# Weight conversion in an attention and MLP kernel: four raw buffers, conversions laid across two pairs, and another queue for stores of x's rows

## Chip, cores and metric

The kernel runs on one core of a Trainium2 chip. The metric is the device time of one execution in microseconds (us), lower is better. A core has five engines with instruction streams of their own: TensorE (PE in the profile; its weight loads are PEld), VectorE (DVE), ScalarE (ACT), GpSimd (POOL) and SyncE (SP), which here only issues DMA transfers. ScalarE and GpSimd can issue them too. "SPq L252" in a profile is an instruction of SyncE's queue from line 252 of the kernel. A queue is worked off in order: an instruction that waits holds up all behind it.

## What is computed

An attention block in which each query sees only the keys of its own cluster, and then a feed-forward block with a residual. Cut to what matters:

```python
def _attn_ref(q, k, v, centroids):          # q, k, v: (4, 8, 768, 64) float32
    q_assign = argmax(q_n @ c_n)            # 16 clusters for each head
    k_assign = argmax(k_n @ c_n)
    mask = q_assign[:, :, :, None] == k_assign[:, :, None, :]
    scores = where(mask, scale * q @ k.T, -1e9)
    return softmax(scores) @ v

def _moe_ref(x, g_ln, w_ch1, w_ch2):        # x: (4, 768, 512)
    xn = (x - mean(x)) / sqrt(var(x) + 1e-06) * g_ln
    return x + maximum(xn @ w_ch1, 0) @ w_ch2
```

The inputs are float32, except the weights `w_ch1` (512 x 2048) and `w_ch2` (2048 x 512). These reach the kernel as 64-bit floating-point numbers. The kernel reads them as pairs of 32-bit words and puts float32 weights together with integer operations.

## The kernel before

**Attention.** The work goes by 16 pairs of heads (4 batches, 4 pairs each); L740 is the loop over the pairs, `n` its index. For each pair TensorE makes masks and scores (L398), ScalarE the exponentials (L393), TensorE the weighted sums of v (L410). VectorE adds the exponentials up (L445 to L449), transposes q and k (L295) and finds the clusters. For batches 0 and 1 `rows_out` (L513) also transposes a pair's result and stores it as rows of x to `x_d` in four DMAs of 96 KB; for batches 2 and 3 this waits until later, and only the columns are stored, to `xT_d` (L504).

**Conversion of the weights.** There are 32 chunks of 128 x 512 weights: 0 to 15 of `w_ch1`, 16 to 31 of `w_ch2`. `load_weight(m)` (L244) brings a chunk's raw words, 512 KB, into a buffer with the tag "raw" (4 KB on each of 128 partitions). `split_weight(m)` (L259) is three VectorE instructions (L265, L268, L271). `join_weight(m)` (L275) is two (L282, L283) and a DMA from GpSimd's queue that adds the low part onto the float32 weight (L286, `w<-tb`). After the join the raw buffer is free, and the call that follows loads chunk m + 2 into it, as there are two raw buffers. In the attention `weight(n, part)` (L733) converts one chunk in each of the pairs 0 to 14, and a second one at the end of the pairs in `TWICE`. That makes 19 chunks; the other 13 are converted in the first stage of the MLP.

**The MLP of batch 0, first layer** (`first_units`, L1325). Each product of matrices is done by a scheme with seven half-size products instead of eight. A unit `j` is seven products of four matmul records; units 1 to 7 follow each other. VectorE adds up the weights that the next unit needs as `ws` (`w1_sums`, L646, instructions at L658), adds PSUM results (L876), and converts the chunks that the list in L841 gives the unit: one in unit 1, two in each of the units 2 to 7. Here the raw, "ta" and "tb" buffers lie in a pool `rest` (L832).

**The MLP of batch 0, second layer** (L1362 to L1421). Seven parts of three row tiles each (L953). `add_rows` (L960) loads a tile of x's rows (`xb`, four buffers) and adds it to the product into `o_sb` (tag "o", nine buffers). In between come jobs for the next batches. Among them `turn_columns` (L1375) transposes a pair of batch 2 or 3 from columns (`col`) to rows (`turned`, one buffer) and stores it with four DMAs (L518). These tiles live in a pool `early`.

**The MLP of batches 1 to 3.** Units as before (L1490), and behind each unit of batch 1 `unit_end` (L1428) turns the remaining pairs and prepares quarter blocks of the second layer's weights (`w2_split`, L1046, instructions at L1053; its source for the blocks 4, 5, 6 and 7 comes back from DRAM by `w2_back`, L1030, into a single buffer). `leaving` (L1188) is a list of stores whose DMA instructions are issued later, by `leave(n)` (L1204).

**Order.** A `manual_schedule` fixes the order on the engines it names as the program has it; on others a scheduler orders the instructions by simulated time. SyncE's order is fixed in the first lines of the attention (L691) and from L1423 on, and left to the scheduler in the attention's loop, in the first layer of batch 0 and in the second layer of batch 0. ScalarE's is left to it only in the second layer of batch 0. The pools lie on a stack in SBUF: `rest` is closed at L1364, and `ffn` and `early` are opened in its place and beyond. A tile there waits until what lay at its place before is no longer used.

Of the kernel before, what the change touches and what calls it, by code (L numbers as in the profile page):

```python
# [8 lines left out]
F32 = mybir.dt.float32  # L9
# [14 lines left out]
def kernel(  # L24
# [11 lines left out]
    nc = tc.nc  # L36
    B, H, S, D = q.shape
    NCL = centroids.shape[1]
    DM, FF = moe_w_ch1.shape
    P = 128  # L40
# [14 lines left out]
    xpool = ctx.enter_context(tc.tile_pool(name="xpool", bufs=1))  # L55
# [10 lines left out]
    conv = pool("conv", 1)  # L66
# [13 lines left out]


    LATER = 2
    TWICE = (1, 10, 11, 12)


    def load_blocks(n, name):
# [142 lines left out]
    WC = 512  # L229
    NW1 = NDC * FF // WC  # L230
    NWC = NW1 + NFC
    raws = {}
    least = const.tile([P, NWC], F32, name="least")
    limit = [NWC]
# [9 lines left out]
    def load_weight(m):  # L244
        if m < NWC and m < limit[0]:
            if limit[0] < NWC:

                raw = xpool.tile([P, 4, NDH, P], F32, tag="ws", name="raw", bufs=2)
                raw = raw.rearrange("p i c f -> p (i c f)").bitcast(mybir.dt.int64)
            else:  # L250
                raw = pools["conv"].tile([P, WC], mybir.dt.int64, tag="raw", name="raw", bufs=2)
            nc.sync.dma_start(out=raw, in_=weight_chunk(m)[0])  # L252
            raws[m] = raw

# [255 lines left out]
        else:  # L510
            late.pop(n)

    def rows_out(b, pr, x, y):  # L513

        nc.vector.transpose(y, x)
        for i in range(P // Q):
            m = pr * P + i * Q
            nc.sync.dma_start(  # L518
                out=x_d[b].rearrange("t (a r) m -> r (t a) m", r=Q)[:, :, m : m + Q],
                in_=y[i * Q : (i + 1) * Q].rearrange("r (g f) -> r g f", f=Q),  # L520
            )
# [2 lines left out]
    asked = list(turning)  # L524
    columns = {}

    def columns_load(tile_of):
        if asked:
            b, pr = asked.pop(0)
            columns[b, pr] = tile_of()  # L530
            nc.sync.dma_start(out=columns[b, pr], in_=xT_d[b][pr])

    def columns_turn(tile_of):
        b, pr = turning.pop(0)
        rows_out(b, pr, columns.pop((b, pr)), tile_of())


    stat_d = [spill.tile([2, S], F32, name=f"stat_d{b}") for b in range(B)]
# [143 lines left out]

    convert = {}
    for n in range(len(pairs) - 1):
        for part in (0, 1) if n in TWICE else (0,):
            convert[n, part] = len(convert)

    pieces = [(0, 0, 0), (1, 0, 0), (1, 1, 0), (0, 1, 0), (1, 0, 1), (1, 1, 1), (0, 0, 1)]
# [34 lines left out]
    with tc.manual_schedule(engines=order | {mybir.EngineType.Pool}):  # L723
        def extras(n, at):
            for job in extra.pop((n, at), ()):
                job()

        def turn_pair(n):
            for side in (1, 0):
                prep_transpose(n, side)  # L730
                load(n + 1, "qk"[side])

        def weight(n, part):  # L733
            m = convert.get((n, part))
            if m is not None:
                split_weight(m)
                join_weight(m)
                load_weight(m + 2)

        for n in range(len(pairs)):  # L740
            nxt = n + 1 < len(pairs)
            own = range(2 * NT * n, 2 * NT * (n + 1))
            if n == 0:
                turn_pair(1)
            elif nxt:
                prep_route(n + 1)
            load(n + 1, "v")
            for i in own:
                if i >= AHEAD:
                    scores(i)  # L750
                if n == 0 and i + 1 == NT:
                    prep_sims(1)
                    prep_route(1)
            extras(n, "scores")
            if 1 < n and nxt:
                finish(n - 2, 1)
            if n and n + 2 < len(pairs):
                turn_pair(n + 2)
            if not nxt:
                finish(n - 1, 1)  # L760
            add_up(n, 0)
            extras(n, "sums")
            if not nxt:
                finish(n - 2, 2)
                finish(n - 2, 3)
            if n and nxt:
                finish(n - 1, 0)
            if nxt:
                for piece in pieces[:4]:
                    prep_mask(n + 1, *piece)  # L770
            add_up(n, 1)
            if n == 0:
                turn_pair(2)
            for i in own[:NT]:
                weigh(i)
            if nxt:
                for piece in pieces[4:]:
                    prep_mask(n + 1, *piece)
            weight(n, 0)
            if n > 1 and nxt:  # L780
                finish(n - 2, 2)
                finish(n - 2, 3)
            extras(n, "weigh")
            for i in own[NT:]:
                weigh(i)
            if n + 2 < len(pairs):
                prep_sims(n + 2)
            elif nxt:
                finish(n, 0)
            weight(n, 1)  # L790
            extras(n, "end")
            if n + 2 == len(pairs):
                finish(n - 1, 1)
            if not nxt:
                for part in (2, 3):
                    finish(n - 1, part)
# [34 lines left out]
    rest, first = ExitStack(), ExitStack()  # L831
    pools["conv"] = rest.enter_context(tc.tile_pool(name="rest", bufs=1))  # L832
    limit[0] = NWC
    for m in range(len(convert), min(len(convert) + 2, NWC)):
        load_weight(m)

    within = {}
    for m in range(len(convert), NWC):
        within.setdefault((1, 2, 2, 3, 3, 4, 4, 5, 5, 6, 6, 7, 7)[m - len(convert)], []).append(m)
    MH = DM // 2  # L840
    hidden = {}  # L841

# [117 lines left out]
    def add_rows(b, r, tt, j, bank):  # L960

        x = early.tile([P, MH], F32, tag="xb", name="xb", bufs=4)
        nc.sync.dma_start(out=x, in_=x_d[b][r * TH + tt, :, j * MH : (j + 1) * MH])
        o = early.tile([P, MH], F32, tag="o", name="o_sb", bufs=9)
        nc.vector.tensor_tensor(o, bank[:, :MH], x, ALU.add)
        return o

# [236 lines left out]
    def leave(n, queues=(nc.sync,)):  # L1204
        for i, (to, y) in enumerate(leaving[:n]):
            queues[i % len(queues)].dma_start(out=to, in_=y)
        del leaving[:n]
# [117 lines left out]
    def first_units(b, j):  # L1325

        chunks = within.pop(j, []) if b == 0 else []
        for part, ahead in ((1, 0), (2, 0), (4, 1), (6, 0), (3, 1), (5, 0), (7, 0)):
# [6 lines left out]
            if chunks and part in (2, 3):  # L1335
                m = chunks.pop(0)
                join_weight(m)
                load_weight(m + 2)

            if part == 5 and j + 1 < NFH:  # L1340
                w1_sums(b, j + 1)
# [20 lines left out]
    with tc.manual_schedule(engines={mybir.EngineType.PE, mybir.EngineType.DVE}):  # L1362
# [10 lines left out]
            return early.tile([P, S], F32, tag="col", name="col", bufs=2)  # L1373

        def turn_columns():  # L1375
            columns_turn(lambda: early.tile([P, S], F32, tag="turned", name="turned", bufs=1))
            if len(turning) > 4:
                columns_load(column)

        def keep(i, t):  # L1380
            return lambda: w2_keep(i, st["t", t])
# [41 lines left out]
    with tc.manual_schedule(engines=order | {mybir.EngineType.SP}):  # L1423
# [4 lines left out]
        def unit_end(b, j):  # L1428
# [4 lines left out]
                if j < NT:  # L1433
                    norm_rows(b + 1, j)
            if b == 1:
                def row():
                    return xpool.tile([P, S], F32, tag="row", name="col", bufs=2)

                if turning and j % 2:
                    columns_turn(row)  # L1440
                elif asked and j % 2 == 0:
                    columns_load(row)
                if j == 0:
                    outer["ends"] = all_in_range()
                if j == 2:
# [17 lines left out]
            if b + 1 < B and j + 2 == NFH:  # L1463
                norm_stat_rows(b + 1)
            leave(4)
            if j > 4:
                for _ in range(4):
                    if ring["next"] < len(STEPS) * (b - 1) + RING:
                        ring_load(b)
# [261 lines left out]
```

## Time and profile before

| what | value |
|---|---|
| three runs | 904.64, 903.95, 903.05 us; median 903.95 us |
| the profiled execution | 904.72 us, of which the instructions' span is 902.8 us |
| TensorE clock granted, mean | 0.993 of full |
| busy: PE, PEld, DVE, ACT, POOL | 97%, 64%, 78%, 45%, 9% |
| DMA | 151.01 MB, 167 GB/s mean |

The span by stage (us of the span; busy us of the engines; the mean busy share of the 16 DMA engines):

| stage | from, to | length | PE | DVE | ACT | PE clock | DMA |
|---|---|---|---|---|---|---|---|
| attention | 0, 318.3 | 318.3 | 315.5 | 286.3 | 256.7 | 1.00 | 0.78 |
| batch 0, first layer | 318.3, 409.0 | 90.7 | 81.8 | 64.6 | 26.7 | 0.96 | 0.69 |
| batch 0, second layer | 409.0, 480.8 | 71.8 | 69.4 | 52.5 | 2.4 | 1.00 | 0.70 |
| batch 1, first layer | 480.8, 557.8 | 77.0 | 75.8 | 58.8 | 35.8 | 1.00 | 0.70 |
| the rest | 557.8, 902.8 | 345.0 | 334.1 | 242.4 | 81.2 | 0.99 | 0.53 |

TensorE is busy nearly all the time, so other engines' time counts only where TensorE waits for it. A line of a timeline has the start in us, the length in us, the engine, the source line, the operation, the tiles written and read, their shape and the number of instructions; in brackets stands how long the engine had been idle before it, and what ended that.

### The profile page before, as it was taken

The page shows a single profiled execution, that of the slowest core. Times are in us where ns is not written, and L with a number is a line of the kernel's source. Part 1 is how long each engine was busy: PE and PEld are TensorE (multiplying, and loading weights), DVE is VectorE, ACT ScalarE, POOL GpSimd, SP SyncE. Part 2 cuts the span into 40 slices and gives each one's busy share as a digit, 9 for nine tenths or more (in the row PEclk, how much of TensorE's full clock was granted, in tenths as well). Part 3 has the DMA queues.
Part 4 walks back from the last instruction along what each step waited for, and adds up shares of the span by engine and source line. Part 5 has one row for each costly group of instructions (what it writes and reads, how often), then busy time and mean ns, then how long its engine had stood idle before and what let it go on. Part 6 is the DMA issues. An engine that isn't in the chain of part 4 may idle for free.

```text
span 902.8 us, 13188 instructions
## 1 busy us (share of the span) xinstructions
PE 876.6 (97%) x4644; PEld 575.4 (64%) x4644; DVE 704.5 (78%) x1149; ACT 402.8 (45%) x739; POOL 77.4 (9%) x143
## 2 busy tenths in 40 slices
PE   9999999999999998989989999999999999999995
PEld 5444444444444455548876556997557997557995
DVE  6899998999998876868657887897646897645774
ACT  6777889888898623221002552102553101333110
POOL 1022111112222202110000000000000000000000
PEclk9999999999999999999999999999999999999998
DMA  7777989988994247867675778963235862421874
GB/s 160 137 145 137 168 153 192 172 168 173 196 195 130 66 150 193 247 170 235 172 185 164 230 232 284 330 196 88 50 84 170 286 204 59 86 84 36 269 201 94
DMA packets 251642, 151.01 MB, mean 167 GB/s; under 512 B 193696, under 2 KB 209200, under 8 KB 250544
## 3 DMA queue, kind: packets, MB, share of 16 engines
q1 hardware_dynamic: 235936, 133.90, 56.7%
q0 software_dynamic: 7776, 15.03, 8.4%
q10 hardware_dynamic: 7856, 1.16, 0.8%
q8 instruction: 39, 0.64, 0.3%
q14 instruction: 35, 0.29, 0.1%
HBM read 108.40 MB, written 33.25 MB: 157 GB/s over the span
## 4 chain that ended last, share of the span: by engine, by line
PE 81%; DVE 7%; DMA 7%; SPq 2%; issue 2%; ACT 1%; DVEq 0%; ACTq 0%; POOLq 0%
PE s_ps L398 16%; PE x_ps L845 13%; PE a_ps L410 13%; PE x_ps L1136 12%; PE z_ps L845 7%; PE z_ps L1136 6%; PE y_ps L845 3%; DMA raw<-in_moe_w_ch_dram 3%; PE y_ps L1136 3%; PE x_ps L953 2%; PE den_ps L466 1%; PE sim_ps L317 1%; PE y_ps L953 1%; PE z_ps L953 1%; DVE lower L876 1%
## 5 line engine op out<-in xcount | busy, mean ns | idle before, releaser
L398 PE MATMUL s_ps<-t,t 64*128 64x384 f32 x768 | 154.8, 483 | 0.0
L398 PEld LDWEIGHTS s_ps<-t,t 64*128 64x128 f32 x768 | 68.0, 187 | 39.0 <-issue 38.3
L1136 PE MATMUL x_ps<-lower,w 128*128 128x192 f32 x448 | 80.9, 327 | 0.9 <-DVE u L1151 0.9
L1136 PEld LDWEIGHTS x_ps<-lower,w 128*128 128x128 f32 x448 | 74.0, 190 | 2.9 <-DVE u L1151 1.5
L876 DVE TENSOR_TENSOR lower<-z_ps,u 128x384 f32<-128x384 f32 x56 | 31.0, 553 | 52.7 <-PE z_ps L845 45.1
L884 ACT ACTIVATE lower<-lower 128x384 f32<-128x384 f32 x88 | 45.5, 522 | 59.0 <-DVE lower L876 59.0
L393 ACT ACTIVATE e<-s_ps 128x768 f32<-128x768 f32 x84 | 67.0, 811 | 7.0 <-PE s_ps L398 6.4
L393 ACT ACTIVATE w<-s_ps 128x768 f32<-128x768 f32 x80 | 64.4, 811 | 8.3 <-PE s_ps L398 7.7
L398 PE MATMUL s_ps<-mask,mask 64*128 64x384 bf16 x384 | 62.8, 323 | 1.0 <-ACT e L393 0.6
L871 ACT COPY u<-x_ps 128x384 f32<-128x384 f32 x64 | 30.5, 477 | 64.6 <-PE x_ps L845 64.6
L410 PE MATMUL a_ps<-e,v_sb 128*64 128x384 f32 x336 | 57.6, 488 | 0.0
L871 ACT COPY p<-x_ps 128x384 f32<-128x384 f32 x32 | 15.1, 471 | 94.1 <-PE x_ps L845 91.6
L410 PE MATMUL a_ps<-w,v_sb 128*64 128x384 f32 x320 | 55.2, 488 | 0.0
L845 PE MATMUL x_ps<-xt,ws 128*128 128x384 f32 x128 | 48.2, 500 | 5.1 <-DVE ws L658 4.3
L845 PE MATMUL x_ps<-xt,w 128*128 128x384 f32 x128 | 48.0, 498 | 2.8 <-ACT u L871 2.7
L845 PE MATMUL z_ps<-xn,ws 128*128 128x384 f32 x128 | 47.3, 492 | 0.0
L845 PE MATMUL x_ps<-xn,ws 128*128 128x384 f32 x128 | 46.6, 487 | 0.0
L845 PE MATMUL x_ps<-xn,w 128*128 128x384 f32 x128 | 46.6, 487 | 0.0
L845 PE MATMUL y_ps<-xn,w 128*128 128x384 f32 x128 | 46.5, 486 | 0.0
L845 PE MATMUL z_ps<-xt,ws 128*128 128x384 f32 x128 | 46.5, 486 | 0.0
L410 PEld LDWEIGHTS a_ps<-e,v_sb 128*64 128x64 f32 x336 | 23.5, 137 | 31.8 <-issue 30.6
L1241 POOL DMA_DIRECT2D out_dram<-y_end x2 | 1.2, 584 | 486.6 <-DMA out_dram<-y 485.6
(226 smaller groups left out, 1677.9 us busy)
## 6 DMA issues: line engine op xcount, KB each, us to landing
w<-w_d SPq DMA_DIRECT2D x84, 256.0 KB, 3.9
raw<-in_moe_w_ch_dram SPq DMA_DIRECT2D x32, 512.0 KB, 4.4
w<-w_t SPq DMA_DIRECT2D x36, 256.0 KB, 4.9
w<-tb POOLq DMA_DIRECT2D x32, 256.0 KB, 5.5
w_d<-wt SPq DMA_DIRECT2D x7, 1024.0 KB, 5.7
w<-w_all SPq DMA_DIRECT2D x27, 256.0 KB, 3.0
v_sb<-in_v_dram SPq DMA_DIRECT2D x32, 192.0 KB, 3.5
xr<-x_d SPq DMA_DIRECT2D x24, 256.0 KB, 2.8
```

Source lines behind the costliest of these rows:

```text
L317: nc.tensor.matmul(sim[r : r + Q, :HC], cT[:, pr, :, :].rearrange("p j c -> p (j c)"), prepared[n][side][:, g * HC : (g + 1) * HC], start= ...
L393: nc.scalar.activation(e, s[:, :, :HC], AF.Exp, scale=SCALE)
L398: nc.tensor.matmul(s[:, j, :HC], of_keys[:, keys], of_queries[:, o : o + HC], start=part == first, stop=part != first, skip_group_check=True,)
L410: nc.tensor.matmul(acc[j * D : (j + 1) * D, :HC], loaded[n]["v"][:, j, c, :], e[:, j, :], start=(c == 0), stop=(c == NT - 1),)
L466: nc.tensor.matmul(den[r : r + Q, :HC], ones, sums[n, g][h][:, j, :], start=h == 0, stop=h == parts - 1, tile_position=(0, r), skip_group_ ...
L845: nc.tensor.matmul(bank[:, :HC], lhs[:, c, :], rhs[:, c], start=first and c == 0, stop=c == NDH - 1, skip_group_check=True,)
L871: nc.scalar.copy(t, bank[:, :HC])
L876: nc.vector.tensor_tensor(h, bank[:, :HC], other, ALU.add)
L884: nc.scalar.activation(h, h, AF.Relu)
L953: nc.tensor.matmul(bank[:, :MH].rearrange("p (h f) -> p h f", h=2), hidden[lhs + (c,)][:, tt * P : (tt + 1) * P], rhs[:, :, c], start=firs ...
L1136: nc.tensor.matmul(bank, w[:, c, :], a[:, c], start=way in (1, 2, 5) and c == 0, stop=c == NQH - 1, skip_group_check=True,)
L1241: queues[i % len(queues)].dma_start(out=to[:, m : m + Q], in_=y[i * Q : (i + 1) * Q].rearrange("r (t f) -> r t f", f=Q))
```

## The change

Five edits:

1. In the attention the pair 1 leaves `TWICE`, and the pairs 4, 6 and 8 are put into a new list `BEGIN`. In these a second chunk is split at the pair's end and joined in the middle of the next pair, ahead of that pair's own chunk. So 21 chunks are converted in the attention and 11 in the MLP, whose list gives units 3 and 7 one chunk instead of two.
2. In the MLP there are four raw buffers: the first four loads are issued at the start, and each join loads chunk m + 4.
3. In `early` there are two buffers for `turned` instead of one, and eight for `o_sb` instead of nine.
4. In the second layer of batch 0 the stores of the turned rows (L518) and the loads of `col` that follow them go by ScalarE's queue.
5. In the units of batch 1 the turning moves from ahead of `w2_split` to the end of `unit_end`, and its four stores go into `leaving`, from where the `leave(4)` at the next unit's `unit_end` issues them.

```diff
-    TWICE = (1, 10, 11, 12)
+    TWICE = (10, 11, 12)
+    BEGIN = (4, 6, 8)
...
+    RAWS = 4
...
-                raw = pools["conv"].tile([P, WC], mybir.dt.int64, tag="raw", name="raw", bufs=2)
+                raw = pools["conv"].tile([P, WC], mybir.dt.int64, tag="raw", name="raw", bufs=RAWS)
...
-    def rows_out(b, pr, x, y):
+    def rows_out(b, pr, x, y, send=nc.sync.dma_start):
         nc.vector.transpose(y, x)
         for i in range(P // Q):
             m = pr * P + i * Q
-            nc.sync.dma_start(
+            send(
...
-    def columns_load(tile_of):
+    def columns_load(tile_of, send=nc.sync.dma_start):
         if asked:
             b, pr = asked.pop(0)
             columns[b, pr] = tile_of()
-            nc.sync.dma_start(out=columns[b, pr], in_=xT_d[b][pr])
-
-    def columns_turn(tile_of):
+            send(out=columns[b, pr], in_=xT_d[b][pr])
+
+    def columns_turn(tile_of, send):
         b, pr = turning.pop(0)
-        rows_out(b, pr, columns.pop((b, pr)), tile_of())
+        rows_out(b, pr, columns.pop((b, pr)), tile_of(), send)
...
-        for part in (0, 1) if n in TWICE else (0,):
+        for part in (0, 1) if n in TWICE + BEGIN else (0,):
             convert[n, part] = len(convert)
...
         def weight(n, part):
+            begun = convert.get((n - 1, 1)) if part == 0 and n - 1 in BEGIN else None
             m = convert.get((n, part))
+            if begun is not None:
+                weight_end(begun)
             if m is not None:
                 split_weight(m)
-                join_weight(m)
-                load_weight(m + 2)
+                if (part, n in BEGIN) != (1, True):
+                    weight_end(m)
+
+        def weight_end(m):
+            join_weight(m)
+            load_weight(m + 2)
...
-    for m in range(len(convert), min(len(convert) + 2, NWC)):
+    for m in range(len(convert), min(len(convert) + RAWS, NWC)):
         load_weight(m)
...
-        within.setdefault((1, 2, 2, 3, 3, 4, 4, 5, 5, 6, 6, 7, 7)[m - len(convert)], []).append(m)
+        within.setdefault((1, 2, 2, 3, 4, 4, 5, 5, 6, 6, 7)[m - len(convert)], []).append(m)
...
-        o = early.tile([P, MH], F32, tag="o", name="o_sb", bufs=9)
+        o = early.tile([P, MH], F32, tag="o", name="o_sb", bufs=8)
...
-                load_weight(m + 2)
+                load_weight(m + RAWS)
...
         def turn_columns():
-            columns_turn(lambda: early.tile([P, S], F32, tag="turned", name="turned", bufs=1))
+            columns_turn(
+                lambda: early.tile([P, S], F32, tag="turned", name="turned", bufs=2), nc.scalar.dma_start
+            )
             if len(turning) > 4:
-                columns_load(column)
+                columns_load(column, nc.scalar.dma_start)
...
             if b == 1:
-                def row():
-                    return xpool.tile([P, S], F32, tag="row", name="col", bufs=2)
-
-                if turning and j % 2:
-                    columns_turn(row)
-                elif asked and j % 2 == 0:
-                    columns_load(row)
+                leave(4)
...
             leave(4)
+            if b == 1:
+                def row():
+                    return xpool.tile([P, S], F32, tag="row", name="col", bufs=2)
+
+                if turning and j % 2:
+                    columns_turn(row, lambda out, in_: leaving.append((out, in_)))
+                elif asked and j % 2 == 0:
+                    columns_load(row)
```

## The prediction

> **What bounds the kernel now.** I read the page first, then the chain of work that ended last, then the timelines of TensorE, VectorE and SyncE between 318 and 560 us, where the change's MLP parts lie. The chain by engine, from the page:
>
> ```profile
> PE 81%; DVE 7%; DMA 7%; SPq 2%; issue 2%; ACT 1%; DVEq 0%; ACTq 0%; POOLq 0%
> ```
>
> TensorE sets the end; the reader is to look for the stretches in which it is held up. By the slices of the page these lie at the start, near 320 to 410, near 460 and 550, and in the tail. The timeline of TensorE shows them in the middle:
>
> ```profile
> 360.90 2.90 PE L845 MATMUL x_ps<-xt,ws 128*128 128x384 f32 x4 [2.52 <-DVE ws L658]
> ...
> 373.25 1.53 PE L845 MATMUL x_ps<-xt,ws 128*128 128x384 f32 x4 [1.58 <-DVE ws L658]
> ...
> 401.19 0.70 PE L953 MATMUL x_ps<-w,lower 128*128 128x256 f32 x2 [1.01 <-ACT lower L884]
> 404.61 2.70 PE L845 MATMUL x_ps<-xt,w 128*128 128x384 f32 x4 [2.73 <-ACT u L871]
> ...
> 463.42 7.17 PE L953 MATMUL x_ps<-w2t,lower 128*128 128x256 f32 x32 [2.35 <-DVE o_sb L965]
> ```
>
> Undisturbed products start 1.29 us apart. Here they wait for VectorE's sums (L658), or for ScalarE, which waits for VectorE in its turn; and the product after a wait can be slow as well (2.90 and 2.70 us for four records instead of 1.45). VectorE's own timeline says why it was late:
>
> ```profile
> 353.75 0.43 DVE L265 TENSOR_SCALAR ta<-raw 128x512 uint32<-128x512 uint32 x1 [6.70 <-DMA raw<-in_moe_w_ch_dram]
> ...
> 369.13 0.69 DVE L936 TENSOR_TENSOR w2t<-w 128x512 f32<-128x512 f32 x1 [1.78 <-DMA xT_d<-late]
> ...
> 398.49 0.43 DVE L265 TENSOR_SCALAR ta<-raw 128x512 uint32<-128x512 uint32 x1 [5.74 <-DMA raw<-in_moe_w_ch_dram]
> ...
> 462.94 0.42 DVE L965 TENSOR_TENSOR o_sb<-x_ps,xb 128x256 f32<-128x256 f32 x1 [6.20 <-DMA xb<-x_d]
> ...
> 546.72 0.69 DVE L1053 TENSOR_TENSOR wt<-w_t 128x512 f32<-128x512 f32 x1 [3.55 <-DMA w<-w_t]
> ```
>
> The first and third are splits that wait for raw words. The list of the tile `raw` gives a load's time to landing in this stage:
>
> ```profile
> DMA to landing us min/median/max: 3.7/6.5/8.8
> ```
>
> With two buffers chunk m + 2 starts to load only when chunk m is joined. Two chunks then cost their own VectorE work (with the unit's sums and additions, 353.75 to 361.89, 8.1 us) and much of a 6.5 us load, against 9.03 us that TensorE takes for a unit (batch 1's units start 9.03 us apart). The two last VectorE lines are other matters: `xb` and `w_t` transfers that were issued late. SyncE's timeline shows behind what:
>
> ```profile
> 455.06 3.54 SPq L518 DMA_DIRECT2D x_d<-turned  x4
> ...
> 459.21 4.50 SPq L963 DMA_DIRECT2D xb<-x_d  x5
> ...
> 537.99 0.61 SPq L1032 DMA_DIRECT2D w_t<-w_t  x1
> ```
>
> **What the Trainium skill says.** "Perfetto Trace Analysis", section "Optimization Strategy", reads a gap that repeats on an engine that should be saturated as a possible sign of too few buffers; this trace agrees, with waits of 6.70, 0.20, 1.51 and 5.74 us before L265. "DMA: Bandwidth & Descriptors", section "Anatomy of one DMA", puts the wait for a semaphore on the issuing sequencer, ahead of dispatch; so `xb` stands behind whatever a store of `turned` waits for, as at 455 to 459. The same page, "Issuing engines are not separate DMA queues": another issuing engine saves only the sequencer's time, as the transfers share the 16 DMA engines. "TensorE: Matmul & The Clock Gate", section "What's actually happening": the clock is gated by recent activity. The trace agrees in kind: 0.83 granted in the slices 360 to 370 and 400 to 410, where TensorE waited over 2 us, and 1.00 around them.
>
> **The change part by part.**
>
> *Four raw buffers, and 11 chunks instead of 13.* What TensorE loses in this stage: from the product at 325.51 to 408.99 it took 83.48 us. Undisturbed that is one product (1.29), seven units of 9.03 (63.2), two products more (2.6) and a second-layer tile of 16 records at 0.216 (3.45), 70.5 us. Lost: 12.9. By place (lateness of each start against the rhythm before it): around 360.90, 4.6 (2.8 of waiting, 0.25 before it and 1.6 of slow clock); at 373.25, 1.8; at 391.76, 0.4; from 401.19 to 408.99, 6.0 (1.2 and 3.0 of waiting, 1.8 of slow clock). The first and last two follow from raw waits: 11.0 together. With four buffers a load is issued two units, some 18 us, ahead of its use, more than twice the slowest landing (8.8). VectorE needs 8.1 us for a unit with two chunks against 9.03, and about 2.9 less with one (the spacing of the five instructions, 0.34 + 0.60 + 0.60 + 0.34 + 0.69, and small gaps). So it keeps up, and has 3.9 us to spare in unit 3. The place at 373.25 has another cause too: four L936 instructions (2.4 us) and 1.78 us of waiting for a store on SyncE's queue. Without the lateness from 353.75 these 4.2 us meet a lead of about 3.7 us (`ws` is ready at about 9.2 us of a unit and used at 12.9), plus 0.9 of slack; I take half of the 1.8 as gained. Sum 11.9; bounds 8 (both raw waits gone, but a clock loss and the L936 place stay) and 12.9.
>
> *What the larger `rest` does.* Its tiles grow from 14 to 22 KB per partition. In the trace the `xb` loads of the second layer were already issued at 327.61, while `rest` lived, so they lay beyond it. After the change `ffn` (16 KB) no longer covers `rest`, and `xb` may lie where "ta" and "tb" are. Then these loads wait for the last conversions. Cover: unit 7 has its only chunk first, so the conversion ends some 6 us before the stage does; add the landing of `w<-tb` (5.5) and of `xb` (2.8), and the rows come about 2 us after the stage's end and are wanted at 3.45. If SyncE puts the `xn` loads ahead, up to 3 us late; 0 taken, +3 as bound.
>
> *Attention.* Pair 1 loses 2.9 us of VectorE work; the pairs 4, 6 and 8 gain 1.7 (0.42 + 0.68 + 0.68, overlapping a little), and 5, 7 and 9 gain 1.1 (0.42 + 0.69), with one `w<-tb` issue of 0.9 us on GpSimd (busy under 4 of 19.25 us a pair) and one raw load of 512 KB. VectorE has 1.3 to 1.4 us idle in an ordinary pair (its timeline, before L445 at 118.66 and 137.92). So the split leaves it 0.3 us late, which the next pair gives back. Pair 1's full extra chunk held VectorE without a gap for three pairs, and TensorE was busy 10.00 of each 10 us all the while. Cost 0; if the cover were gone 0.3 us a pair, 1 us in all. DMA: two chunks more in 320 us, nothing.
>
> *Second layer of batch 0.* The stores' 20 issues and three `col` loads leave SyncE's queue, and with a second `turned` buffer VectorE loses its waits of 2.43 and 2.15 us before L515. `xb` is then issued as soon as a buffer is free (from 440.6 on, after the addition at 440.27) instead of at 459.21. TensorE's 2.35 us at 463.42 and 0.1 of slow start go. On ScalarE each store costs what SyncE's show, 0.55 us in the middle: 20 x 0.55 + 3 x 0.5 = 12.5 us on an engine with 2.4 busy of 71.8. Behind a store that waits there for its transpose stand the square root (L586) and `st` (L604), whose rows are first used about 10 us later (L615 at 454.96), and the copies of batch 1 from 482 on, after the last store (now 476). Eight `o_sb`: twelve are made, three of the first are free from about 430 on, so none waits. Gain 2.4; bounds 1 and 2.5.
>
> *Units of batch 1.* The `w_t` load of 537.99 lands at 546.7, VectorE waits 3.55 us, and TensorE loses 1.4 at 555.89 and 0.4 around it. Moving the transpose (0.97, spaced 0.89) behind `w2_split` issues that load 0.9 us earlier, and 384 KB of stores no longer run just ahead of it. The stores now come at about 543, where SyncE idles until 549.37, behind the transfer that counts. Gain 1.2; bounds 0.5 and 1.8. Late next: `stat_row`, which needs the store's row buffer, free by about 548 and wanted at 553.85.
>
> Sum: 11.9 + 0 + 0 + 2.4 + 1.2 = 15.5, less 0.5 for the `xb` risk as a mean: 15.0. The profiled execution, 904.72, becomes 889.7; the median of the runs shown is 0.8 lower, so 903.95 becomes 889.0.
>
> **Rivals.** *A, VectorE and SyncE's order take over.* In the first layer SyncE's order is the scheduler's; raw loads stood behind `w_all` stores that wait for `w<-tb` (16.5 us in all between 318 and 490), and L936 stays. For it: VectorE at 8.1 of 9.03. Against: 18 us of lead. Gain 5 of 12.9, then 2.4 + 1.2: 8.6, so 895. *B, everything comes,* the 373.25 place and all of the 1.8 included: 12.9 + 2.5 + 1.8 = 17.2, so 886.8. *C, slower.* Place: SyncE's queue in attention pairs 5, 7 and 9. The load after a begun chunk waits for a join half a pair later; if the scheduler sets it ahead of q and k loads, these start late. They have a pair's lead, 19.25 us, and land in 4 to 6 us each, so it decides from about 10 us of hold. Held a whole pair, 9 us would be lost three times, 27 - 15 = 12 slower: 916. For it: SyncE already waited 42.5 us at L252 for joins, in 15 places. Against: the longest was 4.5, and the load stands behind the q and k loads in the program.
>
> **How the numbers follow.** Forecast 0.60 (its own range 887.5 to 892), A 0.18, B 0.12, C 0.07, and 0.03 that gains and a new wait cancel. The range 886.5 to 895.5 holds the forecast, B and most of A, about 0.85. This kernel's measurement tells 0.2%, 1.8 us, from no change: faster 0.90, same 0.03, slower 0.07.
>
> **What would show it.** Right: no wait over 1 us for raw before L265; batch 0's units 9.03 us apart; a clock of 1.00 there; no 2.35 us before a second-layer product; the L1053 wait under 2.7; attention still ending near 318. Wrong: L265 or L658 waits as long as before, `xb` late right after the first layer, or waits for masks or sums in pairs 5 to 10.

## The result, and the profile after

| | before | after |
|---|---|---|
| runs | 903.05 to 904.64 us, four of them | 887.91 to 889.02 us, four of them |
| median | 903.62 us | 888.71 us |
| profiled execution, and its span | 904.72, 902.8 us | 888.41, 886.6 us |
| TensorE clock granted, mean | 0.993 | 0.997 |

The ratio of the times is 0.9832, with a 95% interval of 0.9815 to 0.9849: 14.9 us faster. Foretold were 889.0 us. In what follows a source line of the kernel after is about 10 higher than the one before in the MLP: L845 became L855, L953 became L963, L1053 became L1063, and L265 became L268.

The chain of waits that ended last, by engine, from the page of the kernel after:

```profile
PE 93%; DMA 2%; DVE 2%; issue 1%; SPq 1%; ACT 1%; POOL 0%; DVEq 0%; ACTq 0%; POOLq 0%
```

It was 81% PE with 7% each of VectorE and DMA. The timeline of TensorE after, at the five places that the prediction quoted (start, length, engine, line, operation, tiles, shape, count):

```profile
358.56 1.45 PE L855 MATMUL x_ps<-xt,ws 128*128 128x384 f32 x4
...
367.59 1.45 PE L855 MATMUL x_ps<-xt,ws 128*128 128x384 f32 x4
...
390.81 3.62 PE L963 MATMUL x_ps<-w,lower 128*128 128x256 f32 x16
394.26 1.45 PE L855 MATMUL x_ps<-xt,w 128*128 128x384 f32 x4
...
445.30 10.52 PE L963 MATMUL x_ps<-w2t,lower 128*128 128x256 f32 x48
```

No line has a bracket any more. The first two starts are 9.03 us apart, the unit's undisturbed length. The second-layer tile of 16 records stands in one piece, and the product behind it starts 3.45 us later, which is 16 times 0.216. The four records that took 2.90 and 2.70 us take 1.45. In the last line 48 records run through where VectorE's `o_sb` held them up for 2.35 us.

From the list of the tile `raw` in this stage after, the time to landing:

```profile
DMA to landing us min/median/max: 3.6/4.2/5.6
```

It was 3.7/6.5/8.8. A single wait for raw words is left, of 1.1 us at the stage's first chunk; it was four, the longest 6.70 and 5.74. VectorE's timeline after shows two more things, one that shrank and one that did not:

```profile
444.79 1.83 DVE L618 TENSOR_TENSOR xn<-xn,stat_row 128x768 f32<-128x768 f32 x2 [4.43 <-DMA stat_row<-stat_d]
...
529.72 0.69 DVE L1063 TENSOR_TENSOR wt<-w_t 128x512 f32<-128x512 f32 x1 [1.31 <-DMA w_t<-w_t]
```

The wait for `w_t` is 1.31 instead of 3.55 us. The wait of 4.43 us for `stat_row` holds nothing up: the 48 records above begin half a microsecond later and run on.

**Where the time went.** Matching TensorE's 4644 matmuls one by one (their order is the same in both kernels) gives the gain by stretch, as the change of each record's start against the other kernel (called its offset below):

| stretch | expected, us | measured, us |
|---|---|---|
| up to the first product after attention | 0 | +0.69 |
| batch 0, first layer, 83.48 before, 70.63 after | -11.9 | -12.85 |
| batch 0, second layer | -2.4 | -2.62 |
| units of batch 1, waits that went | -1.2 | -1.93 |
| units of batch 1, a wait that is new | none named | +1.21 |
| the rest | 0 | -0.65 |
| sum | -15.5, less 0.5 for `xb` | -16.15 |

The profiled spans (902.77 and 886.64) differ by 16.13. Of the first row, 0.56 are there before 16.4 us, where the inputs land. Two profiles of the kernel after differ by nearly as much at that place (0.48), so this need not be the change's. In attention itself the offset stays at 0.56 to 318 us: no cost. Of the last row, 0.73 lie behind the last matmul, in a tail that takes between 8.4 and 9.5 us over the profiles of this document.

The new wait, in TensorE's timeline after:

```profile
544.84 2.84 PE L1146 MATMUL x_ps<-lower,w 128*128 128x192 f32 x16 [0.99 <-DMA w<-w_d]
```

and in that of SyncE's queue after:

```profile
534.58 0.46 SPq L608 DMA_DIRECT2D stat_d<-st  x1
538.94 0.86 SPq L611 DMA_DIRECT2D stat_row<-stat_d  x2
539.85 0.42 SPq L1088 DMA_DIRECT2D w<-w_d  x1
```

The block that TensorE waits for is issued at 539.85, behind two loads of `stat_row`. These wait for the store `stat_d` of 534.58 to land: they go out 4.36 us after it, and for 3.90 of these SyncE issues nothing. Before the change the same order stood there (`stat_d` at 549.86, `stat_row` at 553.85, the block at 554.75). But TensorE, held up by its waits just before, came to the block at 560.46, 5.7 us after its issue, and the order cost nothing. Now it is there 4.0 us after the issue.

**What the two long waits were.** The prediction put them down to the number of raw buffers. SyncE's queue before, in the stretch of both waits, shows a second thing:

```profile
341.62 3.17 SPq L1044 DMA_DIRECT2D w_all<-w  x4
344.89 15.42 SPq L252 DMA_DIRECT2D raw<-in_moe_w_ch_dram  x4
...
388.89 3.32 SPq L1044 DMA_DIRECT2D w_all<-w  x4
392.31 1.99 SPq L252 DMA_DIRECT2D raw<-in_moe_w_ch_dram  x2
```

The list of waits before names what the first group waited for (engine, line, total, times, longest):

```profile
SPq L1044 <- DMA w<-tb: 4.7, 1, 4.7
```

Each long wait ends on a load that stands right behind four stores `w_all<-w` of the second layer's weights. The joins that freed the two buffers are in VectorE's timeline before:

```profile
341.35 0.69 DVE L283 SCALAR_TENSOR_TENSOR tb<-raw,tb 128x512 f32<-128x512 uint32 x1
...
390.13 0.69 DVE L283 SCALAR_TENSOR_TENSOR tb<-raw,tb 128x512 f32<-128x512 uint32 x1
```

The first ended at 342.04, and the load was issued at 344.89, when the four stores, 256 KB each, had been issued; it then took 8.84 us to land. For the second these times are 390.82 and 392.31. So there are three ways to be rid of the wait: more buffers, no need for a second chunk in that unit (units 3 and 7 are where the free slots of the shorter list lie), and no stores there. The experiments take them one at a time.

### The profile page after: what moved, and what is told of

Its sections match the earlier page's. It is cut to its first block, busy times and chain, and to the rows that moved or that the text cites. A ratio compares the mean times of both kernels' runs of the same rounds, so it can differ in the third digit from the quotient of the medians.

```text
span 886.6 us, 13193 instructions
## 1 busy us (share of the span) xinstructions
PE 871.5 (98%) x4644; PEld 575.0 (65%) x4644; DVE 704.6 (79%) x1149; ACT 402.7 (45%) x739; POOL 77.8 (9%) x143
## 4 chain that ended last, share of the span: by engine, by line
PE 93%; DMA 2%; DVE 2%; issue 1%; SPq 1%; ACT 1%; POOL 0%; DVEq 0%; ACTq 0%; POOLq 0%
PE x_ps L855 19%; PE s_ps L401 16%; PE a_ps L413 12%; PE x_ps L1146 12%; PE z_ps L855 9%; PE z_ps L1146 6%; PE x_ps L963 5%; PE y_ps L855 5%; PE y_ps L1146 3%; PE z_ps L963 2%; PE sim_ps L320 1%; PE den_ps L469 1%; PE y_ps L963 1%; DVE es L438 1%; DMA flat<-dsb 1%
## 5 line engine op out<-in xcount | busy, mean ns | idle before, releaser
L886 DVE TENSOR_TENSOR lower<-z_ps,u 128x384 f32<-128x384 f32 x56 | 31.1, 555 | 60.1 <-PE z_ps L855 48.9
L855 PE MATMUL x_ps<-xt,ws 128*128 128x384 f32 x128 | 46.6, 487 | 0.9 <-ACT p L881 0.9
L855 PE MATMUL x_ps<-xn,ws 128*128 128x384 f32 x128 | 46.6, 487 | 0.0
L855 PE MATMUL x_ps<-xn,w 128*128 128x384 f32 x128 | 46.6, 487 | 0.0
L855 PE MATMUL z_ps<-xt,ws 128*128 128x384 f32 x128 | 46.5, 486 | 0.0
L855 PE MATMUL y_ps<-xn,w 128*128 128x384 f32 x128 | 46.5, 486 | 0.0
L855 PE MATMUL x_ps<-xt,w 128*128 128x384 f32 x128 | 46.5, 486 | 0.0
L855 PE MATMUL z_ps<-xn,ws 128*128 128x384 f32 x128 | 46.5, 486 | 0.0
```

Of the source, the lines that this page charges most:

```text
L855: nc.tensor.matmul(bank[:, :HC], lhs[:, c, :], rhs[:, c], start=first and c == 0, stop=c == NDH - 1, skip_group_check=True,)
L886: nc.vector.tensor_tensor(h, bank[:, :HC], other, ALU.add)
```

## Experiments

Each group of runs shared a chip and its runs of the kernel before, whose median moved from 900.05 to 903.62 between groups; every ratio is against the runs beside it. Offsets of TensorE are profile against profile, so each rests on one execution of either kernel.

**Which remedy removes the first layer's loss.** First the kernel after with two raw buffers:

```diff
-    RAWS = 4
+    RAWS = 2
```

> The changed kernel with two raw buffers instead of four; 11 chunks stay in the first layer. If the buffers are what counts (my theory): VectorE waits for raw words again, several us in all, and the first layer of batch 0 is 7 to 11 us longer than in the changed kernel, so 896 to 900. If the two chunks fewer are what counts (rival): at most 3 us longer, 889 to 892.

Measured: 887.57 us (886.96 to 888.22), ratio 0.9852 (0.9816 to 0.9888). That is the time of the change with all its parts (887.59 to 888.71 in three groups), and TensorE's offsets in the first layer do not move at all. The theory that the gain needs four buffers fell. The queue of this kernel:

```profile
337.02 8.92 SPq L255 DMA_DIRECT2D raw<-in_moe_w_ch_dram  x3
352.93 2.79 SPq L1054 DMA_DIRECT2D w_all<-w  x4
355.83 0.79 SPq L255 DMA_DIRECT2D raw<-in_moe_w_ch_dram  x1
```

With one chunk less in unit 3 the scheduler sets the first group at 352.93, 11 us later than before, behind the loads of that stretch. VectorE still waits for raw words, 4.9 us in four places with 2.18 the longest, and TensorE notices none of it. Second, the kernel before with four buffers and its 13 chunks:

```diff
-                raw = pools["conv"].tile([P, WC], mybir.dt.int64, tag="raw", name="raw", bufs=2)
+                raw = pools["conv"].tile([P, WC], mybir.dt.int64, tag="raw", name="raw", bufs=4)
...
-    for m in range(len(convert), min(len(convert) + 2, NWC)):
+    for m in range(len(convert), min(len(convert) + 4, NWC)):
...
-                load_weight(m + 2)
+                load_weight(m + 4)
```

> The kernel before with four raw buffers and nothing else; 13 chunks stay. Theory of the buffers: no wait for raw words over 1 us, and of the 12.9 us lost in the first layer 0 to 2 stay (VectorE has 8.1 of 9.03 us to do in six units, and the L936 place at 373 may remain): 891 to 893. Rival: under half is gained, 897 or more.

Measured: 893.03 us (892.05 to 893.94), ratio 0.9905 (0.9869 to 0.9941). In the first layer it too loses nothing against the kernel after, up to 410 us, though the group of four stores still stands there, at 339.49: the load behind it goes out at 342.37 and is needed later. What this kernel loses comes in the second layer, 4.8 us; in batch 1 it loses 1.4 and gets the same back at the ring loads (the loads of weight blocks, L1088 of the kernel after). Of the 4.8, 4.2 are a wait for `o_sb` at 451.35 and slow records behind it, where edits 3 and 4 are missing. The first 0.55, at 410.72, have another cause: with the larger `rest` and 13 chunks the loads of `xb` go out at 395.17, and VectorE waits 6.19 us for them. So four buffers do it with 13 chunks, and eleven chunks do it with two buffers (edits 3 to 5, whose stages come later, stood in that kernel). Third, the kernel before with its two buffers and 13 chunks, and only the sixteen stores `w_all` moved, to the start of batch 1's first `unit_end`:

```diff
-            (7, 2): [turn_columns, do(norm_apply, 1, 1, 0), w2_whole],
+            (7, 2): [turn_columns, do(norm_apply, 1, 1, 0)],
...
                 if j == 0:
+                    w2_whole()
```

> The kernel before (two raw buffers, 13 chunks) with one thing moved: the 16 stores w_all (L1044), which the scheduler puts in groups of four between the raw loads of the first layer, are issued after unit 0 of batch 1. Theory S: the two long waits for raw words came of these groups, which hold SyncE's queue and fill the DMA engines ahead of a raw load; then of the 12.9 us lost in the first layer at most 3 stay. Theory D: two buffers cannot feed two chunks a unit in any case; then 8 us or more stay. The time itself also holds what the stores do in batch 1, so the first layer's length decides: up to 73.5 us between the products at 325.51 and 408.99 (S), or over 78 (D).

Measured: 895.5 us (894.68 to 900.14), ratio 0.9936 (0.9916 to 0.9955). SyncE's queue and VectorE's longest wait for raw words in this kernel:

```profile
336.54 19.16 SPq L252 DMA_DIRECT2D raw<-in_moe_w_ch_dram  x5
...
361.24 4.46 SPq L252 DMA_DIRECT2D raw<-in_moe_w_ch_dram  x2
...
371.31 12.40 SPq L252 DMA_DIRECT2D raw<-in_moe_w_ch_dram  x4
```

```profile
352.20 0.43 DVE L265 TENSOR_SCALAR ta<-raw 128x512 uint32<-128x512 uint32 x1 [1.77 <-DMA raw<-in_moe_w_ch_dram]
```

The waits are 1.77, 0.59 and 0.20 us instead of 6.70, 5.74, 1.51 and 0.20, and the first layer's loss is gone (12.6 us against the kernel before by 408.35 of its time), with the two buffers and 13 chunks left as they were. This shows that the stores on SyncE's queue made the two loads late. The landing time fell from 6.5 to 5.2 us in the median as well; how much of a wait was the place in the queue and how much the transfer beside a megabyte of stores was not taken apart. In the end only 7.9 us of the 12.6 are left against the profile before. The second layer keeps its wait, and slow records behind it that the kernel before does not have there take 1.7 us; and between 507 and 520 TensorE loses 0.56, 2.47 and 0.77 us, after twelve of the moved stores have held SyncE's queue from 483.09 to 494.05.

**Spreading the conversion over attention.** Chunks at the same pairs, but whole, not begun in one pair and ended in the next:

```diff
-    TWICE = (10, 11, 12)
-    BEGIN = (4, 6, 8)
+    TWICE = (4, 6, 8, 10, 11, 12)
+    BEGIN = ()
```

> The changed kernel with the second chunks of pairs 4, 6 and 8 split and joined in the same pair, at its end. My estimate: VectorE is about 1.5 us late after such a pair and gives it back in the next; TensorE does not wait, and the time is that of the changed kernel within 0.5 us. Rival: laying a conversion across two pairs is what keeps TensorE from waiting in the attention; then TensorE loses 1 us or more in pairs 4 to 9, 890 to 892.

Measured: 888.02 us (887.00 to 888.75), ratio 0.9857 (0.9821 to 0.9893), with TensorE's offset in attention unchanged. Beginning a chunk in one pair and ending it in the next was not needed for the gain. Then six second chunks in six pairs running, with no pair between them:

```diff
-    TWICE = (10, 11, 12)
-    BEGIN = (4, 6, 8)
+    TWICE = (7, 8, 9, 10, 11, 12)
+    BEGIN = ()
```

> The changed kernel with second chunks in the six pairs 7 to 12 one after another instead of 4, 6, 8, 10, 11, 12. VectorE falls about 1.5 us further behind with each pair (2.9 more, 1.4 of slack), 9 us by the end of pair 12. If the lead of masks and sums is near half a pair, as I read the trace (clusters found at a pair's start, masks used at the next one's), TensorE loses 0 to 1 us. If the lead is used up at about 4.5 us, which three pairs in a row reach, it loses 3 to 5 us: 892 to 894.

Measured: 890.20 us (888.54 to 891.54), ratio 0.9876 (0.9838 to 0.9913). Masks and sums of the pairs come in time to the last pair; the price stands behind it. The timeline of TensorE in this kernel:

```profile
323.63 1.88 PE L855 MATMUL x_ps<-xt,ws 128*128 128x384 f32 x4 [2.19 <-ACT p L881]
325.30 2.77 PE L855 MATMUL z_ps<-xt,ws 128*128 128x384 f32 x4
```

GpSimd's queue in this kernel shows how VectorE's lateness reaches TensorE:

```profile
302.65 0.89 POOL L289 DMA_DIRECT2D w<-tb  x1 [3.03 <-DVE tb L286]
303.22 0.89 POOL L480 DMA_DIRECT2D flat<-dsb  x1
```

In the kernel after these stand at 300.34 and 302.12. VectorE's late `tb` makes `w<-tb` late, and a pair's sums (`flat<-dsb`) stand behind it: 1.36 us later against TensorE than in the kernel after. VectorE needs what comes of them before the sum `es` (L438) that ScalarE and then TensorE wait for. It comes to 1.3 us of wait against the kernel after and 1.6 of slow clock, 2.9 in this profile. The size is rough: the four runs spread by 3 us, the profiled one is the slowest of them, and the same wait of TensorE is between 0.3 and 1.7 us in other kernels with the attention of the kernel after. Three second chunks in a row (pairs 10 to 12, in the kernel after and in the one above) cost nothing that shows, six do.

**The stores of x's rows.** Both buffers for `turned`, but SyncE's queue, as before:

```diff
-                lambda: early.tile([P, S], F32, tag="turned", name="turned", bufs=2), nc.scalar.dma_start
+                lambda: early.tile([P, S], F32, tag="turned", name="turned", bufs=2), nc.sync.dma_start
...
-                columns_load(column, nc.scalar.dma_start)
+                columns_load(column)
```

> The changed kernel with the stores of turned rows and the loads of col back on SyncE's queue, two turned buffers kept. If the queue is what counts: xb loads stand behind stores again and TensorE waits 1 to 2.5 us before a second-layer product, 889.5 to 892. If the second buffer alone is enough: within 0.5 us of the changed kernel.

Measured: 889.56 us (889.27 to 890.31), ratio 0.9871 (0.9828 to 0.9913). TensorE waits again before a second-layer tile, at 449.52 for `o_sb`, 1.00 us in its timeline and 1.27 by the offsets, and loses another 0.7 in batch 1, of which no cause was looked for. Of the 2.62 us that edits 3 and 4 give in the second layer together, the queue is thus worth about half here, and the second buffer with the old queue the other half. Then ScalarE's queue with one buffer:

```diff
-                lambda: early.tile([P, S], F32, tag="turned", name="turned", bufs=2), nc.scalar.dma_start
+                lambda: early.tile([P, S], F32, tag="turned", name="turned", bufs=1), nc.scalar.dma_start
```

> The changed kernel with one turned buffer, stores on ScalarE's queue. If the queue is what counts: VectorE waits some 2 us before transposes again, but xb is not held up and TensorE loses nothing; within 0.5 us of the changed kernel. If the buffer counts: VectorE's waits reach the additions behind them and TensorE loses 1 to 2.5 us.

Measured: 896.98 us (894.93 to 899.21, 18 runs), ratio 0.9943 (0.9926 to 0.9960), some 8 to 9 us slower than the kernel after; a loss of that size stood in no expectation. VectorE's timeline in this kernel, from the slowest of the 18:

```profile
445.66 0.98 DVE L518 STREAM_TRANSPOSE turned<-col 128x768 f32<-128x768 f32 x1 [7.04 <-DMA x_d<-turned]
...
468.95 0.56 DVE L886 TENSOR_TENSOR lower<-y_ps,p 128x384 f32<-128x384 f32 x1 [7.83 <-PE y_ps L855]
469.43 0.95 DVE L645 TENSOR_TENSOR xt<-xn,xt 128x768 f32<-128x768 f32 x1
```

and TensorE's:

```profile
473.93 2.90 PE L855 MATMUL x_ps<-xt,ws 128*128 128x384 f32 x4 [5.08 <-DVE ws L661]
```

VectorE waits 7.04 us for its only row buffer. But TensorE loses only 0.9 us there. The larger loss comes of an order: an addition of batch 1 (L886) now stands ahead of three of the four instructions of `x_sum` (L645) and of the sums `ws` (L661), which it follows in the kernel after. That addition needs a product that TensorE makes at 467, so VectorE sits idle for 7.83 us and everything behind it comes late: 5.25 us by the offsets, 2.3 of slow clock after it, and another 3.0 at 554, where the new wait for `w_d` has grown to 2.54. VectorE's order is fixed within this block and within the next, from which the addition comes; why it moved across their border is not known. One buffer less changed not only a wait but an order, so this run does not give the price of the buffer alone.

**The turning in batch 1.** The kernel after with edit 5 undone:

```diff
-                leave(4)
+                def row():
+                    return xpool.tile([P, S], F32, tag="row", name="col", bufs=2)
+
+                if turning and j % 2:
+                    columns_turn(row, nc.sync.dma_start)
+                elif asked and j % 2 == 0:
+                    columns_load(row)
...
-            if b == 1:
-                def row():
-                    return xpool.tile([P, S], F32, tag="row", name="col", bufs=2)
-
-                if turning and j % 2:
-                    columns_turn(row, lambda out, in_: leaving.append((out, in_)))
-                elif asked and j % 2 == 0:
-                    columns_load(row)
```

> The changed kernel with the turning of batch 1 back ahead of w2_split and its stores issued at once. The order alone is worth 1.9 us at the deep layer's start, of which 1.1 is given back at the next product, whose ring load then comes late. So TensorE loses about 1.4 + 0.4 us near the first y product of L1146, and the 1.0 before the ring load w_d goes: 0.5 to 1 us slower than the changed kernel.

Measured: 889.24 us (888.31 to 890.83), ratio 0.9870 (0.9826 to 0.9915). By the offsets it loses 0.31, 1.51 and 0.28 around 540 and gets 1.08 and 0.21 back at the ring loads. So edit 5 removes 2.1 us of waiting and hands 1.3 on to the next wait: 0.8 net. Undone alone it could hardly be told from noise in the time; in the trace it can.

**The new wait.** If it is SyncE's order, another order should remove it. Three kernels: the change again as it is, for its scatter; the four ring loads ahead of `norm_stat_rows`; and the ring loads inside it, between the store and the loads that wait for it.

> The changed kernel once more, beside the next one on the same chip: 888 to 889.5, with the same 1.0 us of waiting for w_d at the fifth product of the deep layer of batch 1.

> The changed kernel with the four ring loads of each unit from 5 on issued ahead of the rows of batch 2's norm (stat_d and stat_row), which hold SyncE's queue for a landing. If that hold is the new wait: the 1.0 us before x_ps of L1146 goes, TensorE's later starts move 1.1 to 1.3 us ahead of the changed kernel's, 0.13%. If the data of w_d itself is late, nothing changes. If the norm's rows become late instead, VectorE waits at batch 2's subtraction (L618) and 0 is gained.

The edit of the second:

```diff
-            if b + 1 < B and j + 2 == NFH:
-                norm_stat_rows(b + 1)
             if j > 4:
                 for _ in range(4):
                     if ring["next"] < len(STEPS) * (b - 1) + RING:
                         ring_load(b)
+            if b + 1 < B and j + 2 == NFH:
+                norm_stat_rows(b + 1)
```

Measured: the change again 888.07 us (887.03 to 888.77), ratio 0.9856 (0.9833 to 0.9880), with the wait at 543.88 as before; ring loads first 889.63 (888.92 to 890.92), ratio 0.9872 (0.9849 to 0.9895). The timeline of SyncE's queue in the latter:

```profile
539.30 0.46 SPq L608 DMA_DIRECT2D stat_d<-st  x1
543.68 0.81 SPq L611 DMA_DIRECT2D stat_row<-stat_d  x2
```

The wait at the ring block is gone, but `stat_row` is issued 5.5 us later than in the change beside it, 3.1 of them against TensorE (this execution lies 2.39 us later from 325 on), and from 549 to 563 TensorE loses 0.30, 1.25 and 0.43 us, 0.98 of it waiting for VectorE's `m` (L1161). By the offsets that is 1.2 gained and 2.0 lost. The order was the cause of the wait; this order was no cure. Last, the version in between, beside the change once more:

```diff
-    def norm_stat_rows(b):
+    def norm_stat_rows(b, between=None):
...
+        if between:
+            between()
...
-                norm_stat_rows(b + 1)
+                norm_stat_rows(b + 1, lambda: ring_loads(b))
...
-            if j > 4:
-                for _ in range(4):
-                    if ring["next"] < len(STEPS) * (b - 1) + RING:
-                        ring_load(b)
+            if j > 4 and (j + 2 != NFH or b + 1 == B):
+                ring_loads(b)
```

> The changed kernel a third time, beside the next one on the same chip: 887.5 to 889.5, the 1.0 us wait for w_d at the fifth product of the deep layer there.

> The changed kernel with the four ring loads of unit 6 issued between the store stat_d and the loads stat_row, where SyncE waits some 3.5 us for a landing. They take about 1.8 us to issue, so neither they nor stat_row are late: TensorE's 1.0 us before the fifth product goes and nothing comes back later, 1 us faster than the changed kernel. If the four loads' 1 MB slows the landing of stat_d, part of it returns at the norm of batch 2, as it did with the loads ahead of both.

Measured: the change 887.59 us (886.90 to 888.61), ratio 0.9855 (0.9829 to 0.9880); ring loads in between 886.74 (885.40 to 886.98), ratio 0.9838 (0.9813 to 0.9864). On SyncE's queue of this kernel:

```profile
534.38 0.47 SPq L608 DMA_DIRECT2D stat_d<-st  x1
534.95 0.94 SPq L1090 DMA_DIRECT2D w<-w_d  x1
535.99 1.61 SPq L1090 DMA_DIRECT2D w<-w_t  x2
537.69 0.43 SPq L1090 DMA_DIRECT2D w<-w_d  x1
539.05 0.80 SPq L613 DMA_DIRECT2D stat_row<-stat_d  x2
```

Four ring loads fill the time in which `stat_d` lands, and `stat_row` goes out at 539.05, against 538.94 in the kernel after. TensorE starts the block that it had waited for 1.13 us earlier against the change beside it, 1.21 with the next record, and only 0.06 of this comes back by the last matmul. Five runs each, which hardly overlap, put it 0.85 us ahead of the change on the same chip: the fastest version here. It is under the 0.2% that this measurement tells apart in one comparison, so the times alone don't show it; the trace shows where it comes from.

## Why the prediction was right, and where its reasons were not

**The sum was right**: 889.7 expected for the profiled execution, 888.41 measured; 889.0 and 888.71 for the medians. All its marks for "right" came, but for one: a wait for raw words is 1.1 us, a tenth over the mark, and TensorE doesn't notice it.

**First layer, 11.9 expected, 12.85 measured.** The stretch and its loss were read rightly, and the term was mis-sized where half of the 1.8 us at 373.25 was left standing. All of it went, also in the kernel with only the stores moved: it was the late start from 353.75. In the kernel with four raw buffers alone VectorE still waits 1.84 us before L936, and TensorE loses nothing there: the four L936 instructions and their wait have room. The step that failed is the cause in between, "With two buffers chunk m + 2 starts to load only when chunk m is joined. Two chunks then cost their own VectorE work ... and much of a 6.5 us load". The kernel with two buffers, 13 chunks and the stores moved loses nothing: its loads land in 5.2 us (median), and VectorE's work of 8.1 us a unit bears that. The two long waits were a symptom of the stores ahead of the loads, and so was part of the 6.5. Rival A had seen those stores, but as a leftover that would still cost after the change. They were the cause, and each of edits 1 and 2 gets round them by itself (with eleven chunks the scheduler sets the first group later, with four buffers the load behind it has time), which is why the two edits aren't additive and why a sum over edits, each taken alone, would have counted 12.9 twice. The reading of the Trainium skill's "Perfetto Trace Analysis", "Optimization Strategy", as a call for more buffers led astray here. The page speaks of the same gap repeating on the engine that should be saturated, and says that it can mean this. Here the gaps were four unlike ones (6.70, 0.20, 1.51 and 5.74 us) on VectorE, which is not that engine, and the runs with two buffers show that it need not mean it.

**`xb`, 0 to +3.** The larger `rest` did delay the loads, from 327.61 to 390.32; with two raw buffers, and so the smaller `rest`, they go out at 327.93. No wait followed: VectorE adds the first rows at 394.5, before the stage's end, and not 2 us behind it as worked out. Nothing of the 0.5 taken off was due. With 13 chunks it would have been: there these loads cost the 0.55 us named above.

**Attention, 0.** Right; whole chunks in the same pairs cost nothing either, so the split in two was not what kept this cost at 0.

**Second layer, 2.4 expected, 2.62 measured.** Right in place and mechanism; the term that was a little short is the loss beside the wait of 2.35, 0.27 for 0.1. The buffer and the queue work together: with both buffers but the old queue TensorE loses 1.27 us again. With the new queue but one buffer it loses 0.9, and an order of VectorE's instructions that was not foreseen makes that kernel 8 to 9 us slower.

**Units of batch 1, 1.2 expected, 0.7 net measured.** The waits that went gave 1.93, over the bound of 1.8. "Late next: `stat_row`" named the wrong tile: `stat_row` came in time for VectorE, and what came late was the block that SyncE issues behind it. A wait for a landing costs whatever is queued behind it, not only the tile that is loaded. That the wait stands on the issuing sequencer, ahead of dispatch, is in the Trainium skill's "DMA: Bandwidth & Descriptors", "Anatomy of one DMA", which the prediction cited for `xb` and did not apply here; 534.58 to 538.94 on SyncE's queue agree with it.

**Rivals.** Of B, everything comes, all three terms came (12.85, 2.62 and 1.93 against 12.9, 2.5 and 1.8), and the new wait of 1.21 took the sum back towards the forecast. That the forecast fits to 0.3 us is thus in part luck: its errors cancel. C, SyncE's queue in attention, did not show: the offset there is constant.

## What to carry to other kernels

Ahead of a late load read its queue, and set its issue time against the moment its buffer came free: a gap between the two is the queue's doing, and moving what stands ahead can then do what another buffer does. Where several edits each remove the same wait, undo them one at a time from the finished kernel as well as adding them one at a time to the old one, for sums over edits mislead there. When a wait for a landing must stand on an issuing queue, put, as in the last experiment, issues that are ready between the store and the loads that need it, rather than ahead of the pair or behind it.

## What was not expected of the hardware

A wait's price was not its length, and what came on top of it was nearly all or nothing. Five waits of TensorE in these profiles are of about the same length. Behind two of them (2.35 us at 463.42 in the kernel before, 2.21 at 517.83 with the stores moved) 0.10 us was lost. Behind the three others (2.26 at 451.35 with four raw buffers alone, 2.12 at 450.58 with the stores moved, 2.19 at 323.63 with six second chunks in a row) 1.6 to 1.8 us were lost, as records started twice as far apart as usual. The granted clock agrees: 1.00 from 460 to 470 in the kernel before, 0.83 from 450 to 460 with four raw buffers alone. Behind waits of 1.7 us and less no such stretch shows; behind those of 2.5 us and more (2.52, 2.73, 2.54 and 5.08) there was one each time, of 1.4 to 2.3 us. So what edits 3 and 4 are worth depends on the rest: 2.62 us from the kernel before, 4.2 at the same tile from the one with four raw buffers. The Trainium skill's "TensorE: Matmul & The Clock Gate", "What's actually happening", says that the clock follows activity in a free-running window, and that the moment of a change depends on where in it the first matmul falls. That a gap's price depends on its place in the window in the same way fits these numbers; no run here shows the window itself.

The kernel before has runs from 897.41 to 907.01 us on one chip (29 of them), the kernel after from 886.90 to 889.02 over three groups (14). Which waits of the former vary from run to run was not looked into.
